# One attention and feed-forward kernel on one core: the feed-forward products in another order in each of four batches

## The chip, the cores and the metric

The kernel runs on one NeuronCore of a Trainium2 chip. The metric is the device time of one execution in microseconds (us). An engine of the core is called by the name that the profile gives it: PE is TensorE (matrix products), PEld its weight loads, DVE is VectorE, ACT is ScalarE, POOL is GpSimd, and SP issues the transfers.

## The reference

There are 8 batches of 8 heads, 576 rows and a head dimension of 64. Each head has 32 pack queries p. The packs attend to k and v, and then q attends to the packed result. The heads stand side by side in a row of 512, and a feed-forward network follows.

```
scale = 1.0 / np.sqrt(q.shape[-1])
p_packed = sm_attn(p, k, v)          # softmax(scale * p k^T) v
out = sm_attn(q, p_packed, p_packed)
x = out.transpose(0, 2, 1, 3).reshape(B * S, H * D)     # 4608 x 512
h = x @ w_in                                            # 512 x 2048
g = np.maximum(h, 0.0) + np.log1p(np.exp(-np.abs(h)))   # softplus
return (g @ w_out).astype(np.float32)                   # 2048 x 512
```

## The kernel before, in words

The kernel goes through the eight batches b, and for each through the 16 blocks f of 128 columns of the hidden layer. One pair (b, f) is a unit of the main loop (line 620). A unit holds three kinds of work on TensorE.

The first product (`gemm1`, lines 481 to 504) makes the hidden block ph of 128 columns by 576 rows, in two halves c of 288 rows. Each half has its own PSUM bank, from a pool `ps_h` of two. The weights w_in are multiplied into the packed values beforehand (`make_m`, once in four units), so that the product is of m with the attention weights. Every factor is split into a high and a low part, and three products stand for one: high by high, high by low, low by high (line 496). Over two groups g of heads that makes six matmuls of 288 columns into each half, twelve in a unit. The half c = 0 is completed first and c = 1 after it.

Softplus follows (`softplus`, lines 516 to 537): on each half ScalarE takes Abs (line 523), Exp (524) and Ln (525), and VectorE adds the maximum of h and zero (line 528). That last instruction is the last reader of the bank of ph. VectorE then splits the result into gh and gl (lines 513 and 514). These are used two units later (LAG = 2).

The second product (`gemm2_tile`, lines 539 to 544) multiplies four tiles t of 128 rows each, gh and gl being stationary, by the high and low parts of w_out, which stream in 512 columns. Each tile has its own accumulator acc[t] in PSUM, which collects over all 16 blocks f; for each tile three matmuls run one behind the other: gh by wo_h, gh by wo_l, gl by wo_h. After the last block `store` (lines 548 to 557) has VectorE copy the accumulator to SBUF (line 550), in one of two buffers, and SP sends it out. The pool `ps_acc` has four banks, so the accumulators of the next batch use those of this one. The rows that are left over (576 is four tiles and 64) of two batches go through one further accumulator, acc_m, after each odd batch (`rests`, lines 559 to 579); it takes a bank of the same pool.

The third kind is the attention of the next batch (`attention`, lines 346 to 431). It is written as a generator of some thirty steps: transposes of k or q (psT, line 239), scores (ps, line 252), transposes of the softmax weights (psa, line 285), the packed product (psp, line 295) and its transpose (psx, line 308). All of them, and `make_m` (psm, line 460), take their PSUM buffers in turn from a pool `ps_m` of two. ScalarE or VectorE copies each result out. After each tile t of the second product, 0.56 of a step falls due (PACE, lines 654 to 657).

The order of TensorE's instructions is the order in which the program issues them: the launch (line 697) holds TensorE to manual scheduling. The other engines' orders are made by the framework's scheduler.

The main loop runs, for one unit: the first product of (b, f) with its softplus; then for t = 0 to 3 a tile of the second product of the unit two before, the attention steps due and a stage of the softplus; then `make_m` where it is due.

Of the kernel before, what the change touches and what calls it, by code (L numbers as in the profile page):

```python
# [9 lines left out]
F32 = mybir.dt.float32  # L10
# [16 lines left out]
def pack_attention_then_softplus_ffn(  # L27
# [10 lines left out]
    nc = tc.nc  # L38
# [3 lines left out]
    P = 128  # L42
# [3 lines left out]
    C = S // 2  # L46
    G = H * J // P
    HG = H // G
    NF = DFF // P
    NT = S // P  # L50
    REST = S - NT * P
    LAG = 2
    MC = 512
# [8 lines left out]
    ps_h = ctx.enter_context(tc.tile_pool(name="ps_h", bufs=2, space=bass.MemoryType.PSUM))  # L62
# [7 lines left out]
    wo_h = const.tile([P, NF, DM], F32R, name="wo_h")  # L70
    wo_l = const.tile([P, NF, DM], F32R, name="wo_l")
# [20 lines left out]
    def load_pack(bg, queues):  # L92

        t = cv.tile([P, H, D], F32, tag="m", name=f"p_{bg}", bufs=1)
        for i in range(BG):
            queues[i % len(queues)].dma_start(
                t[i * J:(i + 1) * J], p[bg * BG + i].rearrange("h j d -> j h d")
            )
        return t

    def pack_transposed(bg, t):
        for o in range(0, H, HG):
            ps = bank(f"ppt_{bg}_{o}")
            for i in range(HG):
                nc.tensor.transpose(ps[:D, i * P:(i + 1) * P], t[:, o + i, :], ident)  # L105
            dst = pT[:, o:o + HG, :].rearrange("x h j -> x (h j)")
            nc.vector.tensor_copy(dst[:D], ps[:D])
            nc.scalar.copy(dst[D:], ps[:D])
# [114 lines left out]
    def busy(n, nm, home=None):  # L223


        if home:
            ps = home[0].tile([P, 512], F32, tag=home[1], name=f"busy_{nm}")
        else:
            ps = bank(f"busy_{nm}")
        for _ in range(n):  # L230
            nc.tensor.transpose(ps[:, :P], ident, ident)
# [201 lines left out]
    def weights(b):  # L433

        at_h = work.tile([P, G, S], F32R, tag="at_h", name=f"at_h_{b}", bufs=1)
        at_l = work.tile([P, G, S], F32R, tag="at_l", name=f"at_l_{b}", bufs=1)
        res[b]["at"] = (at_h, at_l)
        for c in range(2):
            cols = slice(c * C, (c + 1) * C)
            for g in range(G):  # L440
                aT = res[b]["aT"][g, c]
                nc.scalar.copy(at_h[:, g, cols], aT)
                nc.vector.tensor_tensor(  # L443
                    at_l[:, g, cols], aT, at_h[:, g, cols].bitcast(F32), op=ALU.subtract
                )


    def m_cols(b):

        return MC if b else MC // 2  # L450
# [30 lines left out]
    def gemm1(b, f, res):  # L481

        n = m_cols(b)
        halves = res["m"][f * P // n]
        at_h, at_l = res["at"]
        phs = []
        for c in range(2):
            ph = ps_h.tile([P, 512], F32, tag="h", name=f"ph_{b}_{f}_{c}")
            phs.append(ph[:, :C])
            i = 0  # L490
            for g in range(G):
                mh, ml = halves[g * n // MC]
                o = g * n % MC + f * P % n
                ms = slice(o, o + P)
                cs = slice(c * C, (c + 1) * C)
                for x, y in ((mh, at_h), (mh, at_l), (ml, at_h)):
                    nc.tensor.matmul(  # L497
                        ph[:, :C], x[:, ms], y[:, g, cs],
                        start=(i == 0), stop=(i == 3 * G - 1),
                    )  # L500
                    i += 1
                    if (b, f, i) == (0, 0, 1) and c == 0:
                        busy(30, "at_l", (ps_acc, "acc"))
        return phs
# [11 lines left out]
    def softplus(b, f, hv, done):  # L516
        e = work.tile([P, S], F32, tag="e", name=f"e_{b}_{f}")
        es = [e[:, c * C:(c + 1) * C] for c in range(2)]
        parts = [slice(0, S)] if b == 0 else [slice(c * C, (c + 1) * C) for c in range(2)]
        for x in parts:  # L520
            for c in range(2):
                if x.start <= c * C < x.stop:
                    nc.scalar.activation(es[c], hv[c], AF.Abs)  # L523
            nc.scalar.activation(e[:, x], e[:, x], AF.Exp, scale=-1.0)  # L524
            nc.scalar.activation(e[:, x], e[:, x], AF.Ln, bias=1.0)  # L525
            for c in range(2):
                if x.start <= c * C < x.stop:
                    nc.vector.scalar_tensor_tensor(  # L528
                        es[c], hv[c], 0.0, es[c], op0=ALU.max, op1=ALU.add
                    )  # L530
        yield
        yield
        r = (b % 2) * REST
        nc.gpsimd.tensor_copy(rest[:, rest_at(b, f), r:r + REST], e[:, NT * P:])  # L534
        yield
        done[b, f] = halves(f"{b}_{f}")
        split(*done[b, f], e[:, :NT * P])

    def gemm2_tile(acc, gh, gl, f, cs, first, last):
        for i, (x, y) in enumerate(((gh, wo_h), (gh, wo_l), (gl, wo_h))):  # L540
            nc.tensor.matmul(  # L541
                acc, x[:, cs], y[:, f, :],
                start=(first and i == 0), stop=(last and i == 2),
            )

    outv = [out[b * S:(b + 1) * S, :].rearrange("(x s) e -> s x e", s=SI) for b in range(B)]

# [11 lines left out]
    def rests(b):  # L559


        fs = sorted(range(NF), key=lambda x: rest_at(b, x))
        gh, gl = halves(f"{b}_m")
        n = NT // 2
        for i in range(0, NF, n):
            o = rest_at(b, fs[i])
            c = i % NT * P
            cs = slice(c, c + n * P)
            split(gh[:, cs], gl[:, cs], rest[:, o:o + n, :].rearrange("x f j -> x (f j)"))
            if i == 0:  # L570
                yield
                am = ps_acc.tile([P, DM], F32, tag="acc", name=f"acc_{b}_m")
            for t in range(n):
                gemm2_tile(
                    am, gh, gl, fs[i + t], slice(c + t * P, c + (t + 1) * P),
                    i + t == 0, i + t == NF - 1,
                )
        store(am, [(0, b - 1, NT * P, REST), (REST, b, NT * P, REST)], f"{b}_m")
        yield


    order = []
# [34 lines left out]
    gs, acc = {}, None  # L617
    units = [(b, f) for b in range(B) for f in range(NF)]
    ahead, chain, due = iter(()), iter(()), 0.0
    for u in range(len(units) + LAG):  # L620
        if u < len(units):
            b, f = units[u]
            if f == 0:
                if (b + 1) % BG == 0 and b + 1 < B:
                    pack_transposed((b + 1) // BG, pt)
                ahead = attention(b + 1) if b + 1 < B else iter(())
                due = 0.0
            chain = softplus(b, f, gemm1(b, f, res[b]), gs)
            next(chain)
            if f == NF - 1:  # L630
                if (b + 2) % BG == 0 and b + 2 < B:
                    pt = load_pack((b + 2) // BG, (nc.sync,))
                for _ in ahead:
                    pass
                if b + 1 < B:
                    weights(b + 1)
        if u >= LAG:
            b2, f2 = units[u - LAG]
            gh, gl = gs.pop((b2, f2))
            if f2 == 0:  # L640
                acc = [ps_acc.tile([P, DM], F32, tag="acc", name=f"acc_{b2}_{t}") for t in range(NT)]
        last = u >= LAG and f2 == NF - 1 and b2 % 2 == 1
        if last:
            both = rests(b2)
            next(both)
        for t in range(NT):
            if u >= LAG:
                gemm2_tile(
                    acc[t], gh, gl, f2, slice(t * P, (t + 1) * P), f2 == 0, f2 == NF - 1
                )  # L650
                if f2 == NF - 1:
                    store(acc[t], [(0, b2, t * P, P)], f"{b2}_{t}")
            if u < len(units):
                due += PACE
                while due >= 1:
                    next(ahead, None)
                    due -= 1
                if b == 0:
                    cdue += CONV
                    while cdue >= 1:  # L660
                        next(conv, None)
                        cdue -= 1
            next(chain, None)
        if last:
            next(both)
        if u + 2 < len(units):


            nb, c = units[u + 2][0], units[u + 2][1] * P
            if c % m_cols(nb) == 0:  # L670
                make_m(nb, c // m_cols(nb), res[nb])
# [29 lines left out]
```

## Time and profile before

| what | value |
|---|---|
| time, median of 3 runs | 799.0 us |
| the three runs | 799.79, 796.33, 799.0 us |
| span of the profiled execution, first to last instruction | 794.2 us |
| TensorE clock granted, mean | 0.992 of full speed |
| PE busy | 766.6 us |
| DVE busy | 511.3 us |
| ACT busy | 464.8 us |
| first product, matmuls of 288 columns | 1536 |
| second product, matmuls of 512 columns | 1536, and 192 into acc_m |

The profile shows one execution. The page gives its span and no other time for it; the runs' times are taken apart from it. A matmul's row has a start and a duration; the durations of neighbours overlap (394 ns mean for 512 columns), so what a matmul costs TensorE is read from one start to the next. A row of a view names the line, the engine, the operation, the tile written and, behind the arrow, the tiles read. For a matmul, acc<-wo_h,gh reads wo_h as the moving and gh as the stationary operand. Where a row ends in square brackets, these hold the time that the engine sat idle before it and what ended that.

### The profile page before, as it was taken

What the parts mean: (1) busy time and instruction counts of PE and PEld (TensorE: products, weight loads), DVE (VectorE), ACT (ScalarE), POOL (GpSimd) and SP (SyncE); (2) the same over time, 40 slices, a digit from 0 to 9 for tenths busy, and PEclk for the clock granted to TensorE, in tenths of its full rate; (3) what the DMA queues carried; (4) which work ended last, traced back from release to release, by engine and by line L of the source; (5) the groups of instructions that cost most, each with busy time, mean ns of one, the idle gap of its engine ahead of it and who ended that gap; (6) DMA issues with size and microseconds to landing.
All of it is one profiled execution on the core that took longest, in us unless ns stands there. A gap on an engine that the chain in (4) does not pass through costs nothing.

```text
span 794.2 us, 14986 instructions
## 1 busy us (share of the span) xinstructions
PE 766.6 (97%) x5724; PEld 609.0 (77%) x5724; DVE 511.3 (64%) x1168; ACT 464.8 (59%) x1181; POOL 94.2 (12%) x166
## 2 busy tenths in 40 slices
PE   6879988999999999999999999999999999999997
PEld 4656766877788787877788787887888777778886
DVE  2788899754686547765677447764677546765554
ACT  5769887665662755665554555665555465555540
POOL 1415353000000000000000000000000000000010
PEclk9999999999999999999999999999999999999999
DMA  9977784031213121032213112132211210010002
GB/s 229 248 188 178 172 229 112 8 107 31 61 31 83 45 56 48 18 83 61 61 31 84 26 50 60 31 84 61 61 31 42 56 31 2 1 54 1 1 0 67
DMA packets 38216, 56.02 MB, mean 71 GB/s; under 512 B 4864, under 2 KB 31488, under 8 KB 38144
## 3 DMA queue, kind: packets, MB, share of 16 engines
q1 hardware_dynamic: 37600, 54.93, 27.2%
q8 instruction: 45, 0.74, 0.4%
q14 instruction: 27, 0.22, 0.1%
q10 hardware_dynamic: 544, 0.13, 0.1%
HBM read 45.61 MB, written 9.44 MB: 69 GB/s over the span
## 4 chain that ended last, share of the span: by engine, by line
PE 80%; ACT 0%; DVE 0%; issue 0%; ACTq 0%; DVEq 0%
PE acc L541 40%; PE ph L497 23%; PE acc_m L541 6%; PE psm L460 3%; PE ps L252 2%; PE psT_q L239 2%; PE psT_k L239 2%; PE psp L295 1%; PE psa L285 1%; PE psx L308 0%; PE ppt L105 0%; ACT e L525 0%; ACT e L524 0%; ACT e L523 0%; DVE o L550 0%; DVE o_m L550 0%
## 5 line engine op out<-in xcount | busy, mean ns | idle before, releaser
L528 DVE SCALAR_TENSOR_TENSOR e<-ph,e 128x288 f32<-128x288 f32 x256 | 114.5, 454 | 167.5 <-ACT e L525 166.2
L541 PE MATMUL acc<-wo_h,gh 128*128 128x512 f32 x512 | 214.8, 419 | 0.7 <-DVE o L550 0.7
L541 PE MATMUL acc<-wo_l,gh 128*128 128x512 f32 x512 | 201.6, 394 | 0.0
L541 PE MATMUL acc<-wo_h,gl 128*128 128x512 f32 x512 | 201.5, 394 | 0.0
L523 ACT ACTIVATE e<-ph 128x288 f32<-128x288 f32 x256 | 103.0, 403 | 163.1 <-PE ph L497 110.7
L497 PE MATMUL ph<-at_h,mh 128*128 128x288 f32 x512 | 159.0, 311 | 5.4 <-DVE e L528 4.5
L497 PE MATMUL ph<-at_l,mh 128*128 128x288 f32 x512 | 152.2, 297 | 1.4 <-DVE at_l L443 1.2
L497 PE MATMUL ph<-at_h,ml 128*128 128x288 f32 x512 | 152.2, 297 | 0.0
L497 PEld LDWEIGHTS ph<-at_h,mh 128*128 128x128 f32 x512 | 96.8, 189 | 40.0 <-DVE gl L514 14.1
L534 POOL COPY rest<-e 128x64 f32<-128x64 f32 x128 | 47.3, 369 | 599.3 <-DVE e L528 598.5
L541 PEld LDWEIGHTS acc<-wo_h,gh 128*128 128x128 f32 x512 | 96.4, 188 | 23.1 <-issue 9.8
L541 PEld LDWEIGHTS acc<-wo_h,gl 128*128 128x128 f32 x512 | 96.4, 188 | 21.7
L524 ACT ACTIVATE e<-e 128x288 f32<-128x288 f32 (+1 forms) x240 | 109.2, 455 | 3.5
L525 ACT ACTIVATE e<-e 128x288 f32<-128x288 f32 (+1 forms) x240 | 109.7, 457 | 2.0
L541 PEld LDWEIGHTS acc<-wo_l,gh 128*128 128x128 f32 x512 | 96.9, 189 | 9.8
L497 PEld LDWEIGHTS ph<-at_l,mh 128*128 128x128 f32 x512 | 97.0, 189 | 4.5 <-DVE at_l L443 2.3
L497 PEld LDWEIGHTS ph<-at_h,ml 128*128 128x128 f32 x512 | 96.9, 189 | 0.0
L514 DVE TENSOR_TENSOR gl<-e,gh 128x512 fp32r<-128x512 f32 x128 | 88.0, 688 | 6.9 <-DVE gh L513 0.5
L513 DVE CAST gh<-e 128x512 fp32r<-128x512 f32 x128 | 57.8, 452 | 6.2
L475 ACT CAST mh<-psm 128x512 fp32r<-128x512 f32 (+1 forms) x72 | 35.5, 541 | 41.2 <-PE psm L460 40.8
L476 DVE TENSOR_TENSOR ml<-psm,mh 128x512 fp32r<-128x512 f32 (+1 forms) x72 | 42.7, 622 | 21.8 <-ACT mh L475 21.7
L460 PE MATMUL psm<-w_in_sb,pt 64*32 64x512 f32 (+1 forms) x576 | 38.6, 553 | 6.3 <-ACT T_q L245 2.1
(75 smaller groups left out, 816.7 us busy)
## 6 DMA issues: line engine op xcount, KB each, us to landing
k<-in_k SPq DMA_DIRECT2D x16, 576.0 KB, 4.6
v<-in_v SPq DMA_DIRECT2D x16, 576.0 KB, 4.5
q<-in_q SPq DMA_DIRECT2D x16, 576.0 KB, 4.9
x_i<-in_moe_w_in SPq DMA_DIRECT2D x32, 256.0 KB, 5.9
x_o<-in_moe_w_out SPq DMA_DIRECT2D x16, 512.0 KB, 3.7
out<-o SPq DMA_DIRECT2D x24, 192.0 KB, 2.5
out<-o SPq DMA_DIRECT2D x16, 128.0 KB, 2.4
out<-o SPq DMA_DIRECT2D x24, 64.0 KB, 2.8
```

Of the source, the lines that this page charges most:

```text
L460: nc.tensor.matmul(ps[hh * J:(hh + 1) * J, :n], res["pt"][g][o:o + D, hh * J:(hh + 1) * J], w_in_sb[o:o + D, hh, c * n:(c + 1) * n], start ...
L475: nc.scalar.copy(mh[:, cols], ps[:, :n])
L476: nc.vector.tensor_tensor(ml[:, cols], ps[:, :n], mh[:, cols].bitcast(F32), op=ALU.subtract)
L497: nc.tensor.matmul(ph[:, :C], x[:, ms], y[:, g, cs], start=(i == 0), stop=(i == 3 * G - 1),)
L513: nc.vector.tensor_copy(hi, x)
L514: nc.vector.tensor_tensor(lo, x, hi.bitcast(F32), op=ALU.subtract)
L523: nc.scalar.activation(es[c], hv[c], AF.Abs)
L524: nc.scalar.activation(e[:, x], e[:, x], AF.Exp, scale=-1.0)
L525: nc.scalar.activation(e[:, x], e[:, x], AF.Ln, bias=1.0)
L528: nc.vector.scalar_tensor_tensor(es[c], hv[c], 0.0, es[c], op0=ALU.max, op1=ALU.add)
L534: nc.gpsimd.tensor_copy(rest[:, rest_at(b, f), r:r + REST], e[:, NT * P:])
L541: nc.tensor.matmul(acc, x[:, cs], y[:, f, :], start=(first and i == 0), stop=(last and i == 2),)
```

## The change

Four batches each get another order of the same matmuls; no matmul is added or taken away.

- Batch 2, first product: the matmuls of the two halves alternate. Both PSUM banks are taken at the start, and each stationary tile is used for c = 0 and then c = 1.
- Batch 3, second product: the tiles 0 and 1 alternate matmul by matmul, then the tiles 2 and 3. Six matmuls run together where t is 0 and where t is 2; none where t is 1 or 3.
- Batch 4, second product: each tile's order becomes gh by wo_h, gl by wo_h, gh by wo_l.
- Batch 5, second product: all four tiles alternate; the twelve matmuls run where t is 0, and none at the other three.

The loop around them stands: attention steps still fall due after each t. The remaining batches are as before. The second product of a batch runs two units behind, so that the batch 5 form, say, holds from the unit f = 2 of batch 5 to f = 1 of batch 6.

```
         phs = []
+        if b == 2:
+            phs = [
+                ps_h.tile([P, 512], F32, tag="h", name=f"ph_{b}_{f}_{c}")[:, :C] for c in range(2)
+            ]
+            i = 0
+            for g in range(G):
+                mh, ml = halves[g * n // MC]
+                o = g * n % MC + f * P % n
+                for x, y in ((mh, at_h), (mh, at_l), (ml, at_h)):
+                    for c, ph in enumerate(phs):
+                        nc.tensor.matmul(
+                            ph, x[:, o:o + P], y[:, g, c * C:(c + 1) * C],
+                            start=(i == 0), stop=(i == 3 * G - 1),
+                        )
+                    i += 1
+            return phs
...
-    def gemm2_tile(acc, gh, gl, f, cs, first, last):
-        for i, (x, y) in enumerate(((gh, wo_h), (gh, wo_l), (gl, wo_h))):
+    def gemm2_tile(acc, gh, gl, f, cs, first, last, by_moving=False):
+        order = ((gh, wo_h), (gh, wo_l), (gl, wo_h))
+        if by_moving:
+            order = ((gh, wo_h), (gl, wo_h), (gh, wo_l))
+        for i, (x, y) in enumerate(order):
...
+    def gemm2_tiles(accs, gh, gl, f, t0, first, last):
+
+        for i, (x, y) in enumerate(((gh, wo_h), (gh, wo_l), (gl, wo_h))):
+            for t, acc in enumerate(accs, t0):
+                nc.tensor.matmul(
+                    acc, x[:, t * P:(t + 1) * P], y[:, f, :],
+                    start=(first and i == 0), stop=(last and i == 2),
+                )
...
         for t in range(NT):
             if u >= LAG:
-                gemm2_tile(
-                    acc[t], gh, gl, f2, slice(t * P, (t + 1) * P), f2 == 0, f2 == NF - 1
-                )
+                n = {3: 2, 5: NT}.get(b2, 1)
+                if n == 1:
+                    gemm2_tile(
+                        acc[t], gh, gl, f2, slice(t * P, (t + 1) * P), f2 == 0, f2 == NF - 1, b2 == 4
+                    )
+                elif t % n == 0:
+                    gemm2_tiles(acc[t:t + n], gh, gl, f2, t, f2 == 0, f2 == NF - 1)
                 if f2 == NF - 1:
                     store(acc[t], [(0, b2, t * P, P)], f"{b2}_{t}")
```

## The prediction

> **What bounds the kernel now.** I read the page first: the busy times, the chain that ended last, and the costliest groups.
>
> ```profile
> span 794.2 us, 14986 instructions
> PE 766.6 (97%) x5724; PEld 609.0 (77%) x5724; DVE 511.3 (64%) x1168; ACT 464.8 (59%) x1181; POOL 94.2 (12%) x166
> PE 80%; ACT 0%; DVE 0%; issue 0%; ACTq 0%; DVEq 0%
> L541 PEld LDWEIGHTS acc<-wo_l,gh 128*128 128x128 f32 x512 | 96.9, 189 | 9.8
> ```
>
> TensorE (PE) is busy for 97% of the span and no other engine has a share worth a percent in the chain. So what lengthens or shortens TensorE's own queue moves the end. There is one weight load for each matmul (5724 and 5724), and wo_l,gh, which follows wo_h,gh with the same stationary tile, still has its 512 loads: a repeated stationary operand is loaded again.
>
> Then the chain in order of time, in stretches without attention work (start, length, what):
>
> ```profile
> 727.52 1.59 PE ph L497 x12
> 770.58 8.18 PE acc L541 x36
> 778.77 11.01 PE acc_m L541 x48
> ```
>
> That is 132.5 ns for a matmul of 288 columns, and 227 and 229 ns for one of 512. The difference, 94.5 ns over 224 columns, is 0.42 ns a column, which leaves about 11 ns for each matmul that no column explains. Which order could touch those 11 ns is seen in the timeline of one unit:
>
> ```profile
> 720.26 0.39 PE L541 MATMUL acc<-wo_h,gh 128*128 128x512 f32 x1
> 720.49 0.40 PE L541 MATMUL acc<-wo_l,gh 128*128 128x512 f32 x1
> 720.73 0.39 PE L541 MATMUL acc<-wo_h,gl 128*128 128x512 f32 x1
> 720.96 0.40 PE L541 MATMUL acc<-wo_h,gh 128*128 128x512 f32 x1
> ```
>
> From start to start it is 0.23 us where the stationary tile repeats (.26 to .49), 0.24 where both operands change (.49 to .73), and 0.23 where the moving operand repeats and the PSUM bank changes (.73 to .96). TensorE asks for its columns and for nothing that an order could save. **So the products themselves cost the same in any order, and the change is worth only what it does to the work between them.**
>
> **Batch 4** (gh,wo_h; gl,wo_h; gh,wo_l): the same three matmuls in the same place. gl is needed one matmul (0.23 us) sooner, but it was made two units before. Zero.
>
> **What stands between the products.** The attention of the next batch is dealt out in steps, 0.56 of one after each tile of the second product, which is 2.24 in a unit. What a step costs TensorE:
>
> ```profile
> 386.06 0.41 PE L239 MATMUL psT_q<-ident,q 96*128 96x96 f32 x3
> 386.26 0.48 PE L541 MATMUL acc<-wo_h,gh 128*128 128x512 f32 x1
> 386.57 0.40 PE L541 MATMUL acc<-wo_l,gh 128*128 128x512 f32 x1
> 387.49 0.39 PE L541 MATMUL acc<-wo_h,gl 128*128 128x512 f32 x1
> 387.81 0.72 PE L252 MATMUL ps<-T_q,pt 64*32 64x288 f32 x16
> ```
>
> After three transposes the next product starts its follower 0.31 us later and not 0.23: the way back costs 0.08. The way into scores costs 0.32 - 0.23 = 0.09 as well. Merging steps saves some of these; what it takes away is the cover. Two buffers of PSUM serve all steps, ScalarE (ACT) and VectorE empty them, and a step often reads the copy that the step before it made:
>
> ```profile
> 539.90 0.41 PE L239 MATMUL psT_k<-ident,k 96*128 96x96 f32 x3
> 540.42 0.39 ACT L245 COPY T_k<-psT_k 128x288 f32<-128x288 f32 x1
> 540.97 0.72 PE L252 MATMUL ps<-T_k,pT 64*32 64x288 f32 x16
> 541.61 0.50 PE L541 MATMUL acc<-wo_h,gh 128*128 128x512 f32 x1
> 541.75 0.70 ACT L261 COPY a<-ps 128x288 f32<-128x288 f32 x2 [0.59 <-PE ps L252]
> 543.10 0.49 PE L285 MATMUL psa<-ident,a 128*96 128x128 f32 x3
> 544.70 0.46 ACT L286 COPY a1T<-psa 96x384 f32<-96x384 f32 x1
> ```
>
> The copy of a transpose is done 0.52 + 0.39 = 0.91 us after the transposes start; the scores that read it follow, with a tile of the second product (0.69) between. Without that tile they could start 0.2 + 0.1 us after the transposes: a wait of 0.6. The first copy out of the scores is done half of 0.70 into its row, about 1.15 us after the scores start, and the scores last 0.64 (540.97 to 541.61): a step that needs their buffer right behind them waits 0.5.
>
> **Batch 5, four tiles together.** All twelve matmuls of a unit run first, then all its steps back to back. From 0.56 a tile and the list of steps, the units f=2 to f=13 hold (transposes T, scores s, a1 transposes a, packed p, pt x; m is make_m): s T m; T T; T s a; a p; T a m; a x; T p T; T s; x T m; T T; T s; none. T s occurs three times: 3 x 0.6 = 1.8. A step behind s twice: 2 x 0.5 = 1.0. The packing in a p reads the copy just asked for (0.46 long): its second half waits some 0.25. make_m needs both buffers, one just filled: about 0.15, 0.4 and 0.4. That is 4.0 us of waits. Saved are 15 returns to the second product at 0.08 to 0.09, 1.3 us. Net 2.7; the ends are 0 (ACT and VectorE run their copies just in time) and 4.5 (no switch saved, copies behind other work).
>
> There is a second place. The first unit of a batch needs the four accumulators, and they come free as VectorE copies them out:
>
> ```profile
> 525.90 0.38 PE L497 MATMUL ph<-at_h,mh 128*128 128x288 f32 x1
> 527.57 0.39 PE L541 MATMUL acc<-wo_h,gh 128*128 128x512 f32 x1
> 528.61 0.69 DVE L550 COPY o<-acc 128x512 f32<-128x512 f32 x1 [1.99 <-DMA out<-o]
> 529.22 0.45 DVE L528 SCALAR_TENSOR_TENSOR e<-ph,e 128x288 f32<-128x288 f32 x1
> 529.77 0.69 DVE L550 COPY o<-acc 128x512 f32<-128x512 f32 x1
> 530.69 0.48 PE L541 MATMUL acc<-wo_h,gh 128*128 128x512 f32 x1
> ```
>
> The third tile's copy waits for a store to land, the fourth stands behind softplus work and ends at 530.46; tile 3 of the next batch starts at 530.69. With four tiles alternating, tile 3 is asked for three matmuls after 527.57, at 528.26: a wait of 2.2 us, or 1.5 if the store lands early and only the softplus work stands ahead. I take 1.9. At the other end of the batch the last tiles finish together and acc_m wants the first one's bank 0.7 us after its last matmul: a copy of 0.69 and its delays, 0.2. **Batch 5: 2.7 + 1.9 + 0.2 = 4.8 us.**
>
> **Batch 3, two tiles together.** Steps still fall after each pair, so mostly one at a time. Only T s (twice, 2 x 0.6) and T p (no dependence) merge, and make_m loses its cover three times (0.1 each): 1.5, less six saved returns (0.5): 1.0. Tile 3's accumulator is asked for two matmuls sooner, or about 0.7; by the rows above that would wait some 0.5 if the copies come as late as there, else nothing. I take 0.2. **Batch 3: 1.2 us**, from 0.3 to 2.
>
> **Batch 2, halves alternate.** Both halves end together, and the first is complete five matmuls (0.66 us) later, so the whole softplus chain starts that much later. Both PSUM banks are asked for at the start of the next first product. Who is late is seen where the units are shortest:
>
> ```profile
> 318.05 0.29 PE L497 MATMUL ph<-at_h,mh 128*128 128x288 f32 x1
> 319.10 0.41 ACT L523 ACTIVATE e<-ph 128x288 f32<-128x288 f32 x1 [2.99 <-issue]
> 319.57 0.45 ACT L331 ACTIVATE a<-a 128x288 f32<-128x288 f32 x1
> 322.14 0.42 DVE L528 SCALAR_TENSOR_TENSOR e<-ph,e 128x288 f32<-128x288 f32 x1
> 322.41 0.30 PE L497 MATMUL ph<-at_h,mh 128*128 128x288 f32 x1
> 270.02 0.41 PE L239 MATMUL psT_k<-ident,k 96*128 96x96 f32 x3
> 270.54 0.39 ACT L245 COPY T_k<-psT_k 128x288 f32<-128x288 f32 x1
> 271.09 0.71 PE L252 MATMUL ps<-T_k,pT 64*32 64x288 f32 x16
> ```
>
> At f=13 the second half's bank is free at 322.56 and asked for at 322.41 + 0.79. Moved by 0.66 it is free at 323.22 and asked for at 322.54: a wait of 0.7, or 0.4 if the exponential of the attention (319.57) slips in ahead of the chain. At f=4 and f=12 the T copy stands in ACT's queue behind part of the softplus; moved, it ends 0.66 later, and the scores, which have it only 0.16 us early now (271.09 less 270.93), wait 0.5, or 0.2 if ACT takes the copy first. The other units are longer, (97.75 - 11) / 16 = 5.4 us on average by the first row below against 4.36 here, and leave about a microsecond more.
>
> ```profile
> 235.35:333.10 97.75, 97.75 (x728) 78.23 (x726) 61.32 (x146) 52.62 (x141) 5.65 (x17) 1.00 0.20 51
> 419.20:516.16 96.96, 96.96 (x720) 77.52 (x718) 60.48 (x144) 52.40 (x141) 6.12 (x17) 1.00 0.19 51
> 516.16:602.18 86.02, 86.02 (x671) 68.53 (x670) 54.27 (x127) 52.23 (x141) 5.93 (x17) 1.00 0.20 54
> ```
>
> (The rows are batches 2, 4 and 5, from the start of the first product to that of the next batch: window, length, then each engine's busy time. Batches 2 and 4 hold the 11 us of acc_m.) **Batch 2: 1.4 us**, from 0.8 to 2.
>
> [...]
>
> **The sum.** 1.4 + 1.2 + 0 + 4.8 = 7.4 us; I call it 7. The page gives the profiled execution's span alone, 794.2 us; the runs shown go from 796.33 to 799.79 with a median of 799.0, so 2 to 6 us lie around the span, untouched by the change. On the median: 806.
>
> **Rivals.**
> *Not slower.* The returns saved outweigh the waits. The instruction orders of ACT and VectorE are not written by hand, so they can be set anew: the fourth accumulator copy ahead of the softplus work (its 1.5 to 2.2 us go), T copies first. Then the waits of the merged steps (4.0 and 1.5) stand against 21 returns; at 0.17 (way in and way out of scores) these give 3.6. Net 0 to 3 us, 799 to 802. It decides if fewer than half of the waits appear. For it: today's copies do start within 0.6 us of their data; against: a dependence of 0.91 us does not shrink. Chance 0.28.
> *Faster.* The 11 ns that no column explains go where neighbouring matmuls share an operand or change bank. The four batches hold 4 x 192 = 768 such matmuls: up to 8.4 us, 791. Against: the three spacings above. Chance 0.06. [...]
> *Slower by more.* In batch 2 every unit pays the 0.66 us, because ACT's order is fixed and everything behind the softplus chain moves: 10.6 in place of 1.4, 815. It decides where a unit's bank comes free less than half a microsecond ahead, as at f=13; a unit of average length has a microsecond more. Chance 0.06.
> That the change doesn't do what it says is hardly open: TensorE's order is the one written down, and loads are not merged today.
>
> **How the numbers follow.** The forecast has 0.60, its own range 802 to 811 (sum of the low ends 0.8 + 0.3 + 1.7 and of the high ends 2 + 2 + 7). A difference of 0.5%, 4 us, is about what a measurement of this kernel can tell from none. Faster by more: 0.06. Slower by more: most of the forecast and the last rival, 0.62. Within: 0.32. The range takes in part of the first rival: 800 to 812.
>
> **What would show it.** Matmul spacings 0.23 and 0.13 in all batches. Batch 4 takes its 96.96 us again within 0.3. Batch 5 goes from 86.02 to some 91, with TensorE waiting for T copies (L252), for accumulators in its first unit (about 2 us); batches 2 and 3 one to two more each, batch 2 at f=13 waiting for VectorE's L528. I am wrong if batch 5's units are no longer than before, or if a matmul's spacing moves.

## The result and the profile after

| | before | changed |
|---|---|---|
| median of 4 runs each | 799.39 us | 809.69 us |
| the runs | 796.33 to 805.64 us | 808.56 to 809.92 us |
| span of the profiled execution | 794.2 us | 806.8 us |
| ratio, 95% interval | | 1.0119 [1.0075, 1.0163] |

The change made the kernel slower by 1.2% by the ratio, 10.3 us by the medians (the kernel before has one run more than in the first table) and 12.6 us by the two spans. Each run of the changed kernel is 1.8 us longer than its own span (808.56 and 806.8 in the profiled one); by the same 1.8 us the profile before shows an execution of some 796 us, shorter than the median run, so its span flatters the old kernel. The page of the changed kernel, the lines that answer to those of before:

```profile
span 806.8 us, 14972 instructions
PE 775.5 (96%) x5724; PEld 612.9 (76%) x5724; DVE 512.0 (63%) x1168; ACT 465.0 (58%) x1181; POOL 94.4 (12%) x166
PE 78%; ACT 2%; DVE 1%; issue 0%; DVEq 0%; ACTq 0%
```

The same 5724 matmuls and 5724 weight loads, and the same work on the other engines to within 1 us. TensorE is idle for 31.3 us of the span in place of 27.6; its busy time grew by 8.9 us without a matmul more, since a matmul's row, or a group's, also holds waits between its parts (the scores of one unit of batch 2 take 1.43 us where they take 0.72 without the wait) and runs longer at a lower clock (four matmuls take 1.87 us at half clock and 1.07 at full; all four rows stand below). ScalarE and VectorE have come into the chain that ended last. So waits were added, not work.

Each batch is cut out from the start of its first product to that of the next batch. Window, length, and each engine's busy time; the clock granted to TensorE is the column of 1.00 and 0.98. Before, the two batches that the prediction doesn't show:

```profile
333.10:419.20 86.10, 86.10 (x673) 68.60 (x671) 54.56 (x127) 53.01 (x142) 5.97 (x16) 1.00 0.21 54
602.18:699.14 96.96, 96.96 (x720) 77.52 (x718) 60.43 (x144) 52.41 (x141) 6.13 (x17) 1.00 0.10 27
```

After, batches 2 to 6:

```profile
235.61:335.32 99.71, 99.60 (x727) 78.45 (x726) 59.93 (x145) 49.66 (x141) 5.37 (x17) 1.00 0.20 50
335.32:424.03 88.71, 88.71 (x674) 70.01 (x671) 55.77 (x128) 54.89 (x142) 6.34 (x16) 1.00 0.20 53
424.03:520.97 96.94, 96.94 (x719) 77.52 (x718) 60.34 (x144) 52.36 (x141) 6.10 (x17) 1.00 0.19 51
520.97:614.37 93.40, 90.25 (x672) 70.76 (x670) 55.01 (x127) 53.83 (x141) 6.23 (x17) 0.98 0.19 50
614.37:711.56 97.19, 97.10 (x719) 77.61 (x718) 60.46 (x144) 52.16 (x141) 6.10 (x17) 1.00 0.10 27
```

Batch 2 takes 1.96 us more, batch 3 2.61, batch 4 nothing, batch 5 7.38, and batch 6, which holds the end of batch 5's second product, 0.23. That is 12.2 of the 12.6 us; the rest lies in the start and in the batches 0, 1 and 7, which the change does not touch.

Outside batch 0 a unit of this kernel repeats from profile to profile within some 0.03 us, so I give below, for a unit, the time from the start of its first product to the start of the next, less the same of the kernel before.

- Batch 2: f=0 +0.32, f=4 +0.72, f=12 +0.72, f=14 +0.24, all others within 0.04.
- Batch 3: f=2 +0.50, f=4 +0.60, f=6 +0.60, f=10 +0.51, f=12 +0.61, the others between -0.11 and +0.06.
- Batch 5: f=2 +4.39, f=4 +1.04, f=5 +0.27, f=6 +0.56, f=9 +0.50, f=10 +0.48, f=12 +0.47, the others between -0.17 and +0.10.

One unit of batch 5 lost more than the other fifteen. Its second product in the timeline (a row of x4 is four matmuls):

```profile
532.38 0.62 PE L569 MATMUL acc<-wo_h,gh 128*128 128x512 f32 x2
533.88 0.50 PE L569 MATMUL acc<-wo_h,gh 128*128 128x512 f32 x1 [0.87 <-DVE o L578]
535.05 0.50 PE L569 MATMUL acc<-wo_h,gh 128*128 128x512 f32 x1 [0.68 <-DVE o L578]
535.39 1.09 PE L569 MATMUL acc<-wo_l,gh 128*128 128x512 f32 x4
536.32 1.87 PE L569 MATMUL acc<-wo_h,gl 128*128 128x512 f32 x4
538.11 1.21 PE L252 MATMUL ps<-T_k,pT 64*32 64x288 f32 x16
539.84 0.47 PE L239 MATMUL psT_k<-ident,k 96*128 96x96 f32 x3 [0.52 <-ACT a L261]
```

Tile 2 would have come at 532.84 and comes at 533.88 (1.04 late); tile 3 then at 534.11 and comes at 535.05 (0.94 late). Both wait for the copy of the old accumulator. That is the forecast wait, 1.98 us. What was not forecast stands below it: the four matmuls at 536.32 last 1.87 and not 1.09, the scores 1.21 and not 0.72. The same stretch by microseconds, with the granted clock as the column before the DMA share:

```profile
536.00:537.00 1.00, 1.00 (x5) 0.82 (x4) 0.55 (x1) 0.00 (x0) 0.00 (x0) 0.68 1.03 312
537.00:538.00 1.00, 1.00 (x3) 0.36 (x2) 0.00 (x0) 0.00 (x0) 0.00 (x0) 0.50 0.65 246
538.00:539.00 1.00, 1.00 (x17) 0.23 (x16) 0.00 (x0) 0.00 (x0) 0.00 (x0) 0.50 0.01 2
539.00:540.00 1.00, 0.48 (x10) 0.16 (x3) 0.00 (x0) 0.61 (x2) 0.00 (x0) 0.62 0.00 0
```

The clock, full before and after these rows, stood at half for (0.32 + 0.5 + 0.5 + 0.38) x 2 = 3.4 us behind the wait.

My theory after this: the order costs nothing; what costs is that steps lost the products between them, that accumulators are asked for sooner, that the softplus chain of batch 2 starts later, and that the wait may have lowered the clock (0.50 for 3.4 us behind it, in one profile so far). The rival: alternating tiles or PSUM banks costs by itself.

### The profile page after: what moved, and what is told of

The parts are those of the page before. It is cut to its first block, busy times and chain, and to the rows that moved or that the text cites. A ratio compares the mean times of both kernels' runs of the same rounds, so it can differ in the third digit from the quotient of the medians.

```text
span 806.8 us, 14972 instructions
## 1 busy us (share of the span) xinstructions
PE 775.5 (96%) x5724; PEld 612.9 (76%) x5724; DVE 512.0 (63%) x1168; ACT 465.0 (58%) x1181; POOL 94.4 (12%) x166
## 4 chain that ended last, share of the span: by engine, by line
PE 78%; ACT 2%; DVE 1%; issue 0%; DVEq 0%; ACTq 0%
PE acc L560 28%; PE ph L513 19%; PE acc L569 10%; PE acc_m L560 5%; PE psm L460 4%; PE ph L497 3%; PE ps L252 2%; PE psT_q L239 1%; PE psT_k L239 1%; PE psp L295 1%; PE psa L285 1%; ACT e L540 0%; ACT e L539 0%; ACT e L541 0%; DVE e L544 0%
## 5 line engine op out<-in xcount | busy, mean ns | idle before, releaser
L560 PE MATMUL acc<-wo_h,gh 128*128 128x512 f32 x384 | 161.0, 419 | 0.7 <-DVE o L578 0.7
L560 PE MATMUL acc<-wo_l,gh 128*128 128x512 f32 x384 | 151.2, 394 | 0.0
L560 PE MATMUL acc<-wo_h,gl 128*128 128x512 f32 x384 | 151.2, 394 | 0.0
L513 PE MATMUL ph<-at_h,mh 128*128 128x288 f32 x448 | 139.7, 312 | 5.2 <-DVE e L544 4.3
L513 PE MATMUL ph<-at_l,mh 128*128 128x288 f32 x448 | 133.2, 297 | 1.4 <-DVE at_l L443 1.2
L513 PE MATMUL ph<-at_h,ml 128*128 128x288 f32 x448 | 133.0, 297 | 0.0
L513 PEld LDWEIGHTS ph<-at_h,mh 128*128 128x128 f32 x448 | 84.5, 189 | 35.8 <-issue 13.5
L560 PEld LDWEIGHTS acc<-wo_h,gh 128*128 128x128 f32 x384 | 72.6, 189 | 17.3 <-issue 7.0
L560 PEld LDWEIGHTS acc<-wo_h,gl 128*128 128x128 f32 x384 | 72.5, 189 | 14.8
L560 PEld LDWEIGHTS acc<-wo_l,gh 128*128 128x128 f32 x384 | 72.8, 190 | 9.1
```

Source lines behind the costliest of these rows:

```text
L513: nc.tensor.matmul(ph[:, :C], x[:, ms], y[:, g, cs], start=(i == 0), stop=(i == 3 * G - 1),)
L560: nc.tensor.matmul(acc, x[:, cs], y[:, f, :], start=(first and i == 0), stop=(last and i == 2),)
```

## The experiments

Where no time is given below, the kernel ran once and its profile is compared by batches and units; those five runs took 800.11 us (steps back in their places), 806.83 (grouped), 800.54 (one unit), 808.35 (four store buffers) and 807.61 (a copy on the other engine).

**The order alone, everywhere.** The kernel before, all eight batches alternating four tiles, but three matmuls at a time, so that each step keeps its place (the code is put in short):

```
order = [(i, x) for i in range(3) for x in range(t - t % n, t - t % n + n)]
for i, x in order[t % n * 3:t % n * 3 + 3]:      # n = NT where 0 < f2 < NF - 1, else 1
    matmul(acc[x], (gh, gh, gl)[i][tile x], (wo_h, wo_l, wo_h)[i][f])
```

> The kernel before the change with the four-tile alternation in the second product of all eight batches, dealt out three matmuls at a time so that every step keeps its place; the first and the last unit of a batch go tile by tile. The 1344 alternating matmuls share their moving operand with a neighbour in 9 of 12 cases and change bank in 12 of 12. Theory (the order is free): within 1 us of the kernel before, ratio 0.999 to 1.001, and 0.226 to 0.232 us from matmul to matmul. Rival A (the 11 ns per matmul that no column explains go): up to 15 us faster. Rival B (a change of bank costs): the 0.5 us a unit that batch 5 lost on average, 50 us slower.

Measured: 798.2 us against 798.57, ratio 0.9997 [0.9963, 1.0032]. Batches 2, 3 and 5:

```profile
234.71:332.45 97.74, 97.74 (x727) 78.22 (x726) 61.27 (x146) 52.57 (x141) 5.88 (x17) 1.00 0.20 51
332.45:418.56 86.11, 86.11 (x674) 68.60 (x671) 54.57 (x127) 52.96 (x142) 5.90 (x16) 1.00 0.21 54
515.51:601.54 86.03, 86.03 (x672) 68.53 (x670) 54.30 (x127) 52.36 (x141) 5.85 (x17) 1.00 0.20 54
```

These are the lengths of before, 97.75, 86.10 and 86.02, to 0.01 us. From one matmul of the second product to the next it is 0.231 us in the median of each of the batches 1 to 6, as before. With 1344 matmuls in the other order neither the 11 ns went nor was anything added: the order is free. Both rivals fall.

**The changed kernel, steps back in their places.** Batches 3 and 5 are dealt out as above, their first units too.

> The changed kernel, but in batches 3 and 5 the alternating products are dealt out three at a time, so that the attention steps stand between them at the places that they have before the change. Batches are timed from the first product to the next batch's; before 86.1 us in batch 3 and 86.0 in batch 5, changed 88.7 and 93.4. Theory (waits where steps lost their cover, and for accumulators in the first unit): batch 3 falls to 86.1 to 86.3; batch 5 to 86.5 to 87.5, since its third accumulator is still asked for two matmuls after the first (a wait of about 1.0 us) and its fourth right behind the scores. Rival (alternating tiles and banks costs by itself): 88.7 and 93.4 stay within 0.5 us. Batch 2 stays at 99.7 under both.

Measured (batches 3 and 5):

```profile
335.31:421.44 86.13, 86.13 (x673) 68.60 (x671) 55.20 (x128) 53.07 (x142) 5.96 (x16) 1.00 0.21 54
518.40:606.18 87.78, 87.00 (x672) 68.65 (x671) 54.48 (x127) 52.47 (x141) 5.84 (x17) 1.00 0.20 53
```

Batch 3 lost all of its 2.61 us. In batch 5 only the first unit is longer (+1.76, which puts the batch at 87.78, a little over the 86.5 to 87.5 that I had expected); the other units are as before. Batch 2 stayed at 99.71.

**Grouped, not alternated.** The changed kernel, the loops over tiles and over products exchanged:

```
-        for i, (x, y) in enumerate(((gh, wo_h), (gh, wo_l), (gl, wo_h))):
-            for t, acc in enumerate(accs, t0):
+        for t, acc in enumerate(accs, t0):
+            for i, (x, y) in enumerate(((gh, wo_h), (gh, wo_l), (gl, wo_h))):
```

> The changed kernel, but inside each group of two or four tiles the products go tile by tile as before the change; the steps still come after the group. Theory: batch 3 stays at 88.5 to 88.8, since all of its loss is steps without cover. Batch 5 keeps the 3.1 us of its units f=3 to f=13 and about 0.6 at f=2, but asks for the fourth accumulator nine matmuls after the first and not three, so its wait shrinks from 2.0 us to about 0.6 and the clock is not lowered: 90 to 90.5 us in place of 93.4. Rival (the alternation costs by itself): 86.1 and 86.0.

```profile
336.45:425.19 88.74, 88.74 (x674) 70.00 (x672) 55.78 (x128) 54.90 (x142) 6.34 (x16) 1.00 0.21 53
522.13:613.07 90.94, 88.98 (x671) 70.23 (x670) 54.98 (x127) 53.82 (x141) 6.22 (x17) 1.00 0.19 52
```

Batch 3 loses what it lost with the alternation, unit by unit. Batch 5 keeps the losses of f=4 to f=12 to 0.02 us and has +1.92 at f=2 in place of +4.39; with 90.94 it lies 0.4 above the range expected. So the grouping costs 2.6 us in batch 3; in batch 5 the alternation adds the wait for accumulators and what follows it.

**One unit alone.** The kernel before, with the four-tile form in the first unit of batch 5's second product only (`n = NT if (b2, f2) == (5, 0) else 1`, batches 2 and 4 as before).

> The kernel before the change, with the four-tile alternation and its steps behind it in the very first unit of batch 5's second product alone (f=0 of the product, run in the unit f=2); everything else as before. Theory (the wait for two accumulators is 2.0 us, the steps without cover 0.65, and the wait lowers TensorE's clock to half for 3.4 us, some 1.7): that unit takes 4.4 us more, all other units of batches 1 to 7 are as before within 0.1 but for the one after. If the lowered clock hangs on where the wait falls in some period, it is 2.7 with no lowered clock near 535 us. Rival (the loss comes of long stretches of alternation): under 1 us.

```profile
517.65:606.81 89.16, 87.10 (x671) 68.68 (x670) 54.54 (x127) 52.38 (x141) 6.13 (x17) 1.00 0.20 53
```

That unit took +3.14, all others of batches 2 to 6 were as before within 0.02, and the clock stayed at full. It is between my two numbers: 0.4 more than 2.7, and 1.25 less than the 4.39 of the changed kernel. The 0.4 fits the steps: with the wait gone (the run with four store buffers) they cost 1.01 in this unit and not 0.65.

**The changed kernel once more.**

> The changed kernel once more, to see whether the lowered clock in batch 5 comes back. If it belongs to the wait: lowered for 3.4 us in the unit f=2 of batch 5 again, that unit +4.4 us. If it hangs on where the wait falls in a period that the kernel does not set: that unit either +4.4 or, as in the two other runs with the same wait, +3.1, with all other units as in the first profile to 0.1 us.

Its unit f=2 of batch 5:

```profile
533.17 0.62 PE L569 MATMUL acc<-wo_h,gh 128*128 128x512 f32 x2
534.60 0.50 PE L569 MATMUL acc<-wo_h,gh 128*128 128x512 f32 x1 [0.81 <-DVE o L578]
535.75 0.50 PE L569 MATMUL acc<-wo_h,gh 128*128 128x512 f32 x1 [0.66 <-DVE o L578]
536.09 1.09 PE L569 MATMUL acc<-wo_l,gh 128*128 128x512 f32 x4
537.02 1.07 PE L569 MATMUL acc<-wo_h,gl 128*128 128x512 f32 x4
538.02 0.71 PE L252 MATMUL ps<-T_k,pT 64*32 64x288 f32 x16
```

The same two waits (0.81 and 0.66 idle), but the matmuls behind them run at full clock; the unit took +3.02, all others as in the first profile within 0.1. The time was 807.72 us. So I estimate the lowered clock at about 1.3 us (4.39 less 3.02 is 1.37, and 0.09 of it is that the two tiles came 1.98 us late there and come 1.89 late here), and one of the four profiles with this wait has it; one thing that differs between them is shown in the last section.

**Four store buffers.** The changed kernel; `store` takes halves of the two buffers in turn, so that four copies have room.

> The changed kernel with four buffers of SBUF for the copies out of the accumulators (each of the two is cut in halves) in place of two, so that the third and fourth copy need not wait for a store to land. Theory (the first unit of batch 5 waits 2.0 us for two accumulators, and the clock, lowered for 3.4 us behind that, costs about 1.5 more): both go, batch 5 falls from 93.4 to 89.7 to 90.2 us and no lowered clock is left at 536 us. Rival (the lowered clock comes of the alternation or of the steps run together, not of the wait): the waits go but the clock is still lowered, 91.4. Batch 3 stays at 88.7 under both.

```profile
338.24:428.06 89.82, 89.24 (x673) 69.99 (x671) 55.95 (x128) 54.90 (x142) 6.33 (x16) 1.00 0.21 52
525.01:615.06 90.05, 88.43 (x672) 70.42 (x670) 54.87 (x127) 53.82 (x141) 5.96 (x17) 1.00 0.20 52
```

Batch 5 did what I expected (its unit f=2 +1.01 in place of +4.39), and the clock stayed at full there; since it also did so in three of four profiles with the wait, that shows little about the clock. Batch 3 did not: its unit f=2 went from +0.50 to +1.58. The timeline of that unit says why:

```profile
353.38 0.41 PE L239 MATMUL psT_k<-ident,k 96*128 96x96 f32 x3
353.72 1.06 PE L460 MATMUL psm<-w_in_sb,pt 64*32 64x512 f32 x8
354.16 0.77 ACT L272 ACTIVATE a<-a,nm 128x576 f32<-128x576 f32 x1 [1.44 <-DVE nm L267]
354.93 0.38 ACT L245 COPY T_k<-psT_k 128x288 f32<-128x288 f32 x1
355.36 1.06 PE L460 MATMUL psm<-w_in_sb,pt 64*32 64x512 f32 x8 [0.58 <-ACT T_k L245]
```

ScalarE's order was set anew: an exponential (L272) that waits for VectorE now stands ahead of the copy T_k, which frees the buffer for the second half of make_m; in the changed kernel the copy went first (at 350.91 us, the exponential at 351.35). Without cover, TensorE here pays for another engine's order at once, 1.08 us more in this unit.

**A copy on the other engine.** The changed kernel; two T copies of the attention that runs in batch 2 go to VectorE:

```
+        if (b, g, hh) == (3, 1, HG - 1):
+            nc.vector.tensor_copy(dst, ps[:, :C])
+        else:
             nc.scalar.copy(dst, ps[:, :C])
```

> The changed kernel; in the attention of batch 3, which runs during batch 2, two copies of transposes (k and q, second group, last pair of heads) go to VectorE in place of ScalarE. Theory (in batch 2 the units f=4 and f=12 lost 0.72 us each because the copy that the scores need stands in ScalarE's queue behind the softplus chain, which starts 0.66 us later): both fall to 0 to 0.2, batch 2 from 99.7 to 98.3 to 98.7 us. Rival (these two units lose it on the banks of the first product, or to the alternation): they stay at +0.7. The units f=0 (+0.32) and f=14 (+0.24) stay.

The unit f=4 of batch 2, first in the changed kernel:

```profile
270.59 0.41 PE L239 MATMUL psT_k<-ident,k 96*128 96x96 f32 x3
271.28 0.77 ACT L541 ACTIVATE e<-e 128x288 f32<-128x288 f32 x2
271.66 1.43 PE L252 MATMUL ps<-T_k,pT 64*32 64x288 f32 x16
271.94 0.40 ACT L245 COPY T_k<-psT_k 128x288 f32<-128x288 f32 x1
```

and with the copy on VectorE:

```profile
272.28 0.41 PE L239 MATMUL psT_k<-ident,k 96*128 96x96 f32 x3
272.73 0.46 DVE L246 COPY T_k<-psT_k 128x288 f32<-128x288 f32 x1 [2.12 <-PE psT_k L239]
272.97 0.77 ACT L544 ACTIVATE e<-e 128x288 f32<-128x288 f32 x2
273.35 0.72 PE L255 MATMUL ps<-T_k,pT 64*32 64x288 f32 x16
```

The copy starts 0.45 us after the transposes in place of 1.35 (behind both Ln of the softplus chain), and the scores take 0.72 in place of 1.43. Units f=4 and f=12 are at 0.00 and +0.01, and batch 2 at 98.34 us. f=0 and f=14 stay.

**Pairs of independent steps.** If a return to the second product costs 0.08 us and waits come only of dependence, steps that do not need each other should gain by standing together. The kernel before, with yields taken out between such steps (transposes of k and of q by twos, both halves of the softmax weights, the packed transpose with the next packed product), and PACE from 0.56 to 0.375 (one of these places is shown):

```
 for hh in range(HG):
     kT.append(transposed("k", b, 0, hh))
-    yield
+    if not pair or hh % 2:
+        yield
```

> The kernel before the change, products in their old order, with attention steps that do not depend on each other run two at a time (transposes of k and of q in pairs, both halves of the softmax weights, the packed transpose with the next packed product) from batch 1 on; 0.375 of a step falls due per tile, so that they spread over the batch as before and none stands right ahead of the product of m. Theory (a return to the second product costs 0.08 us and needs no cover where the neighbours are independent): 12 returns fewer in each of 7 batches, 7 us; 790 to 795 against 799, ratio 0.990 to 0.996. Rival (two buffers make pairs wait for the copies of the step before, as in the changed kernel): no gain, or up to 3 us slower.

> As the run of pairs, but the due count starts 0.375 lower, so that every step falls one tile later and some stand right ahead of the first product. Theory: the same returns are saved, since a return into the first product costs the same 0.08; within 1.5 us of the run of pairs. Rival (the place in the unit decides, through the copies that the next steps need): more than 2 us apart.

Measured: the first 1.0088 [1.0058, 1.0118], the second 1.0029 [1.0002, 1.0057], both slower. The gain of 7 us that I had expected did not come, and the first lost twice what its rival allowed. Both lost in batch 0 (111.6 us against 106.75 before), where the attention of batch 1 runs among the conversion of the weights. The second gained 0.3 us in each of batches 1 to 6, a third of the 1.0 that I had expected; the first gained as much in batches 2, 4 and 6 and gave more back in batches 1, 3 and 5 (87.77 us in batch 5), where acc_m does not stand between the old accumulators and the new, and the unit f=2 of batch 5 took 1.3 us more, TensorE waiting there for the copies out of the old accumulators (1.11 and 0.36 idle). The two runs lie 3.2 us apart: the place does decide. The last version leaves the attention in batch 0 as it was (`pair = b > 1`, PACE 0.56 while b is 0):

> As the run of pairs shifted, but the attention that runs during batch 0 keeps its single steps and its old pace, since both runs of pairs lost 5 us in batch 0, where weights are still being converted. Theory: batch 0 returns to 106 to 107 us and batches 1 to 6 each stay 0.3 us under the kernel before, 2 us in all; 796.5 to 797.5 against 799, ratio 0.996 to 0.999. Rival (the gain of 0.3 us a batch is bought by work pushed to the next): no difference.

Measured 797.43 us against 799.06, ratio 0.9972 [0.9948, 0.9995]. Batch 3:

```profile
335.93:421.73 85.80, 85.80 (x674) 68.93 (x672) 54.98 (x127) 54.20 (x142) 6.50 (x16) 1.00 0.21 55
```

Each of batches 1 to 6 is 0.3 us shorter than before, 2 us in all. Batch 0 took 108.06 us and not the 106 to 107 expected; the clock granted in it was 0.94 of full speed, before 0.97. The median is 1.6 us below the kernel before, and the interval ends just under 1: if this version is faster, it is by little.

## Why the prediction was right, and where its sizes were off

The sign, the places and the mechanism held; the medians give 10.3 us where I had 7, and the profile 12.6. Without the lowered clock (the second profile of the changed kernel) batches 2 to 6 lost 10.9 us where the terms sum to 7.4: all three terms were too low, and batch 3 with 2.61 us lies above its own range of 0.3 to 2.

- *The order is free.* Held: batch 4 at 96.94, and the run of the order alone, which also settles the rival *Faster*. In batch 2 the alternating matmuls of the first product follow each other at 0.132 us, before 0.133 (medians).
- *Steps that lose their cover, T s.* I had 0.6 less 0.09; batch 3 shows +0.60 and +0.61, batch 5 +0.50 and +0.47. Held. So did the step behind the scores (f=4 of batch 5, T s a: 0.6 + 0.5 forecast less returns, 1.04 measured) and a p (f=5: 0.25, measured 0.27).
- *make_m loses its cover (0.1 each in batch 3; 0.15, 0.4 and 0.4 in batch 5).* This is the term that was mis-sized. In batch 3, f=2, 6 and 10 show +0.50 to +0.60 each, 1.6 in place of 0.3. The stretch of f=6 in the changed kernel:

```profile
374.06 0.49 PE L285 MATMUL psa<-ident,a 128*96 128x128 f32 x3
374.48 1.70 PE L460 MATMUL psm<-w_in_sb,pt 64*32 64x512 f32 x16
374.58 0.47 ACT L286 COPY a1T<-psa 96x384 f32<-96x384 f32 x1 [1.34 <-PE psa L285]
375.11 0.15 PEld L460 LDWEIGHTS psm<-w_in_sb,pt 64*32 64x32 f32 x8 [0.48 <-ACT a1T L286]
376.10 0.40 PE L513 MATMUL ph<-at_h,mh 128*128 128x288 f32 x1
```

The first eight of the 16 matmuls start at once; the weights of the second eight wait for the copy a1T, which frees their buffer, and the next product starts 1.62 us after the first of the 16 (before: 1.02, from 531.56 to 532.58 in the unit f=2 of batch 5). In the run with four store buffers the split is to be seen: eight take 1.06, then eight more take 1.06. Before the change all sixteen took 1.09 in one row (at 348.60, the unit f=2 of batch 3), hardly more than eight alone, so there the two groups ran side by side, and I estimate from these durations that a late second buffer costs up to the whole of the overlap, some 1 us; the prediction gave its 0.1 to 0.4 without working this out. That the two groups overlap is read from these durations, not tested by a run of its own. In batch 5 the units f=2 (with four store buffers), 6 and 10 show +1.01, +0.56 and +0.48 where waits of 0.65, 0.4 and 0.4 were charged ahead of the returns.
- *Accumulators in batch 5.* 1.9 us forecast, 1.98 measured, half of it already at tile 2 and half at tile 3, behind the third and fourth copy as named. In batch 3 I had 0.2; nothing is lost there (the steps-in-place run has f=2 at 0.00).
- *The lowered clock.* Not in the sum at all: 1.3 us in the profiled execution, none in the three other profiles with this wait.
- *Batch 2.* 1.4 forecast, 1.96 measured. f=4 and f=12 cost 0.72 each, where I had 0.5 at most, because ScalarE was also given both Exp and both Ln ahead of the copy (in f=4 from 270.61 and from 271.28 us, the copy at 271.94). f=13, by contrast, cost 0.24 (it shows in f=14), not 0.7 or 0.4. ScalarE took one of the attention's exponentials ahead of the softplus chain and the other behind it (at 321.53 and 323.79 us), and with both halves ready at once the chain had no gap in it; the second bank came free 4.57 us after the start of the unit's first product, where it was 4.51 before. And f=0, +0.32, was not seen: alternating, the second matmul pair asks for the low part of both halves of the attention weights, and the second is still being made (the pair takes 0.71 us where the pair before it takes 0.42, and VectorE makes the low parts from 235.28 to 236.51 us; read from the profile, not tested). A unit does not pay 0.66 us each time: 12 of the 16 are within 0.04 us of before, the later chain being hidden by what remains of the unit. The rival *Slower by more*, which charged all 16, falls.
- *Returns saved.* Units with two independent transposes together are 0.07 to 0.17 us shorter, near the 0.08 forecast. Over a whole batch of pairs the gain was 0.3 us where twelve returns would give 1.0; where the other 0.7 went was not tried. In batch 5 the steps came to 4.0 us (the 6.02 of the second profile less 1.98), as much as the forecast waits before the 1.3 of returns was taken off: its four units of independent steps (f=3, 7, 8 and 11) gave back only some 0.45, and make_m took up part of the rest.
- *Not slower*, the rival that I gave 0.28, falls: it needed fewer than half of the waits to appear, and nearly all did. The other engines' orders were set anew, but the merged steps that read a fresh copy still waited, and in batch 3 of the store-buffer run a new order made it worse.
- *Two figures around the sum.* The high ends 2 + 2 + 7 put the top of the forecast's range at 810 and not 811. And the 2 to 6 us around the span mixed different executions; each run is 1.8 us longer than its own span, and the rest of the spread lies inside the executions.

## What to carry to other kernels

On TensorE, which is the bound here and takes its work in the order written, the order of equal matmuls was worth nothing (ratio 0.9997 with 1344 of them alternating), but the places where other work stands among them were worth much (2.6 us of 86 in batch 3): products between two dependent steps are what hid the copy. Before moving such work, list for each step what it reads and which buffer it takes, and for each accumulator how long after the group's start it is asked for. To find a few microseconds in 800, cut the profile into units that repeat, and compare those.

## What the runs showed of the hardware

A wait of about 2 us in two pieces (0.87 and 0.68 idle, one matmul between them) was followed by a granted clock of 0.50 on TensorE for 3.4 us in one profile, and by the full clock in three others (0.81 and 0.66; 1.08 and 0.46; 1.6 in two pieces in the run with the copies on VectorE). One thing that differs is when the wait came. In the first profile of the changed kernel the clock goes down to 0.50 four times before TensorE's work ends, at 31.18, 58.49, 119.93 and 536.35 us, for 3.41 us each; the last three of these times lie 8, 26 and 148 times 3.413 us behind the first. Cut at this distance, the wait falls into one step. In the second profile, cut where I read such steps from its trace, it falls on two (window, length, TensorE's busy time and so on; the clock as above):

```profile
532.94:536.35 3.41, 1.86 (x8) 1.27 (x8) 3.03 (x6) 1.19 (x4) 0.43 (x1) 1.00 0.91 226
536.35:539.76 3.41, 2.98 (x21) 1.14 (x19) 0.20 (x1) 0.37 (x2) 0.00 (x0) 0.50 0.39 140
530.89:534.30 3.41, 2.90 (x20) 2.34 (x18) 1.74 (x4) 2.05 (x6) 0.00 (x0) 1.00 0.56 141
534.30:537.71 3.41, 2.45 (x10) 1.80 (x10) 2.78 (x6) 0.62 (x2) 0.42 (x1) 1.00 0.96 268
```

The first two rows are the step with the wait and the one behind it in the first profile, the last two the steps of the second. TensorE is idle for 1.55 us of the one step, and for 0.51 and 0.96 of the two. So in this pair of profiles the clock was lowered where the whole wait fell into one step. That is two profiles and no run of its own, and it gives no bound on idle time: a step of the first profile that held 1.41 us of it (130.17 to 133.58) was followed by the full clock.
